# Attention and two expert layers on one core: last queries with the values moving, double transposes, and places that the plan keeps free

## The chip, the core and the metric

The kernel runs as one program on 1 core of a Trainium2 chip. Its engines are TensorE (PE, whose weight loads have a row of their own, PEld), VectorE (DVE), ScalarE (ACT), GpSimd (POOL) and SyncE (SP, which here only issues DMAs). The metric is the device time of one execution in microseconds; of several runs the median counts.

## What is computed

```python
def _attn_ref(q, k, v):            # q, k, v: [4, 8, 576, 64] float32
    q_rot, k_rot = (rotate(q), rotate(k))        # rotary embedding over the position
    scores = scale * np.matmul(q_rot, k_rot.transpose(0, 1, 3, 2))
    scores = scores - np.max(scores, axis=-1, keepdims=True)
    attn = np.exp(scores)
    attn = attn / (np.sum(attn, axis=-1, keepdims=True) + 1e-09)
    return np.matmul(attn, v)
def _moe_ref(x, w_in, w_out):      # 512 -> 2048 -> 512
    h = x @ w_in
    return (h * np.clip(h + 3.0, 0.0, 6.0) / 6.0) @ w_out
def _moe2_ref(x, w_in, w_out):
    h = x @ w_in
    return (h * (1.0 / (1.0 + np.exp(-1.702 * h)))) @ w_out
x = attn_out.transpose(0, 2, 1, 3).reshape(2304, 512)
return _moe2_ref(_moe_ref(x))
```

The weights come as float64. Nothing has to be written out between the three parts.

## The kernel before

**Precision.** Nearly every matrix product is made of numbers cut in two: a rounded high part (names ending in h) and the rest (names ending in l), and three matmuls (high by high, high by low, low by high) stand for one. A few products of attention take the full float32 matmul instead, which needs no low part: which ones is set by the numbers F00 to F21 of the table `C`, read by `full`.

**Attention.** The function `attention` goes over 16 pairs of heads (`pair`, 4 batches of 4 pairs). Of 576 queries 512 are four blocks of 128 for each head, and the last 64 of both heads share one block, whose rows 0 to 63 belong to one head and 64 to 127 to the other. For each block PE makes the scores (L554 for the four blocks, both heads at once, each on half of the array; L541 for the shared block), DVE takes the maximum (L527) and ACT the exponential (L529), which leaves the unnormed weights `P` (128 queries by 576 keys). To multiply by the values, PE transposes `P`, one key block after another (L609: 4 transposes of 128x128, one for each query block, into one of the 8 PSUM banks), ACT copies the high part out (L613), DVE the low part (L630), and PE multiplies (L636; L626 is the full float32 form; L621 the last, half-filled key block). The two halves of the product lie on partitions 0 to 63 and 64 to 127, and are added by `otmp` (ACT) and L643 (DVE) into `xf`.

**The shared last queries.** Their weights are transposed by L576 and L577 (into the banks `T8` and `E`), copied as `P8h` and `P8l` (L581 to L587), and multiplied in `pv8` (L596): the values are the weights of the array, 128 wide, and 64 columns of `P8h` or `P8l` move; 9 matmuls for each head, 18 in all. The halves are added by `otmp8` (ACT) and two L660 (DVE).

**The norm.** POOL spreads the reciprocal sums over 640 columns (`rx`: L400 twice, and L653 for the shared queries), PE transposes these in five pieces (L668 four, L669 one, into `E`), and DVE multiplies `xf` by them (L671, and L673 for the shared queries).

**First expert layer.** `moe1` works for each batch on 512 tokens (the last 64 queries of all batches are gathered in `xt` and run with batch 3 as a block of 256 columns, `xth` and `xtl`). Its 16 blocks of the hidden size go in 8 groups of two: L809 makes h, L814 (ACT) and L816 (DVE) the function, `gh` and `gl` (ACT, POOL) the two parts, L834 the second product, which L843 adds to `y`. The layer of batch b runs while attention of batch b+1 runs, and with batch 3 it runs alone. The first pass converts the weights from float64 (`weights`: SP loads `raw`, then ACT, POOL and DVE) and keeps them in DRAM (`w_hl`); later passes read them back by DMAs that POOL issues (L690).

**What sets the order.** All work is handed to a planner (`Plan`) as steps with an engine, an estimated time and a key. `Plan.run` plays the steps through by these estimates: whenever an engine is free, it takes the step with the lowest key whose inputs are done and whose places (buffers, PSUM banks) are free, and the order in which it took them becomes the order of the program. On the chip each engine then works through its own row strictly in that order and waits where an input is late. The numbers in `C` are keys, estimates and limits.

**The change of places.** After attention its pools (`apool`, `pp`) close, and two new pools take their memory: `y3pool` (yh, yl) and `tpool` (yback, xth, xtl, yt). Three 1 MB results of the first layer, kept in `y_dram`, come back as `yback` (L926), and are cut into `yh` and `yl` for the second layer. The steps of this part are handed over after the first `Plan.run`, and the planner does not know that their memory is attention's until then; the program's dependences still make them wait for it. The second layer (L1019, L1059, L1131) follows, alone on PE, to the end.

## Time and profile before

| | us |
|---|---|
| median of 3 runs | 1160.97 |
| lowest and highest | 1160.32, 1161.18 |
| the profiled execution | 1160.02 |
| its span, first to last instruction | 1158.2 |
| busy: PE, DVE, ACT, POOL | 1113.5, 729.5, 556.2, 650.5 |

The trace is of one profiled execution. The busy time of PE counts the modelled ends of pipelined matmuls, so a busy PE can still start its next matmul late; the distance from start to start of rows in a list in order of time is the surer price. Start times count from the start of the span. PEclk is the mean granted TensorE clock of a stretch, where 1.00 is 2.4 GHz.

### The profile page before, as it was taken

How to read it: one execution, taken by the hardware profiler on the slowest of the kernel's cores; microseconds unless marked ns; L12 is line 12 of the kernel's file. 1: busy time of each engine (PE TensorE's matmuls, PEld its weight loads, DVE VectorE, ACT ScalarE, POOL GpSimd, SP SyncE). 2: the span in 40 equal slices, each digit the busy share in tenths (PEclk: the TensorE clock that was granted, in tenths of full speed). 3: DMA queues.
4: the chain of work that ended last, by engine and by line, in shares of the span. 5: the costliest groups of instructions: out<-in, count | busy, mean ns of one | idle time of the engine just before them, and what ended most of it. 6: DMA issues, size and time to landing. Idle time of an engine off the chain costs nothing.

```text
span 1158.2 us, 17085 instructions
## 1 busy us (share of the span) xinstructions
PE 1113.5 (96%) x6408; PEld 918.1 (79%) x6408; DVE 729.5 (63%) x1131; ACT 556.2 (48%) x1106; POOL 650.5 (56%) x668
## 2 busy tenths in 40 slices
PE   5999999999999999999997999999999999999995
PEld 4667676776888888888886888888888888888884
DVE  5789777887756665566664343566556655565543
ACT  5787866566645554655544432253433334332330
POOL 5777777867753566353433444556745547464440
PEclk9999999999999999999998999999999999999998
DMA  3345565555543456443326543222012010110012
GB/s 90 90 133 169 178 192 188 190 187 184 177 132 103 129 149 182 126 142 109 109 74 218 191 138 109 74 65 81 19 55 61 31 55 19 56 55 25 30 74 91
DMA packets 58891, 129.73 MB, mean 112 GB/s; under 512 B 13752, under 2 KB 26808, under 8 KB 58040
## 3 DMA queue, kind: packets, MB, share of 16 engines
q1 hardware_dynamic: 44712, 78.13, 20.9%
q0 software_dynamic: 13824, 50.34, 14.6%
q8 instruction: 50, 0.82, 0.3%
q14 instruction: 33, 0.27, 0.1%
q10 hardware_dynamic: 272, 0.16, 0.0%
HBM read 103.97 MB, written 24.64 MB: 111 GB/s over the span
## 4 chain that ended last, share of the span: by engine, by line
PE 87%; DVE 5%; POOL 3%; ACT 2%; DMA 1%; issue 1%; SPq 0%; DVEq 0%; POOLq 0%
PE psum L834 17%; PE psum L1131 17%; PE psum L809 15%; PE psum L1019 11%; PE psum L1059 6%; PE psum L609 5%; PE psum L554 4%; PE psum L636 4%; PE psum L596 2%; PE psum L626 2%; DMA raw<-in_moe_w_in_dram 1%; PE psum L541 1%; POOL t L387 1%; DVE sc L527 1%; ACT P L529 1%
## 5 line engine op out<-in xcount | busy, mean ns | idle before, releaser
L387 POOL TENSOR_TENSOR gl<-t,gh 128x512 fp32r<-128x512 f32 (+1 forms) x144 | 183.1, 1275 | 146.3 <-ACT gh L397 126.3
L529 ACT ACTIVATE P<-psum,sc 128x576 f32<-128x576 f32 x144 | 105.4, 739 | 49.9 <-DVE sc L527 49.2
L527 DVE TENSOR_REDUCE sc<-psum 128x1 f32<-128x576 f32 x144 | 102.9, 751 | 30.0 <-PE psum L554 25.6
L1137 DVE TENSOR_TENSOR oacc<-oacc,psum 128x512 f32<-128x512 f32 x124 | 85.0, 685 | 49.0 <-PE psum L1131 47.5
L1131 PE MATMUL psum<-woh,gh 128*128 128x512 f32 x284 | 111.2, 391 | 0.0
L1131 PE MATMUL psum<-woh,gl 128*128 128x512 f32 x284 | 110.8, 390 | 0.0
L1131 PE MATMUL psum<-wol,gh 128*128 128x512 f32 x284 | 110.6, 390 | 0.0
L809 PE MATMUL psum<-xh,wih 128*128 128x512 f32 x256 | 107.1, 418 | 2.5 <-DVE t L816 2.5
L613 ACT ACTIVATE PTh<-psum 128x512 fp32r<-128x512 f32 (+2 forms) x160 | 88.0, 597 | 43.3 <-PE psum L609 42.6
L397 ACT ACTIVATE gh<-t 128x512 fp32r<-128x512 f32 (+1 forms) x136 | 82.2, 606 | 51.0 <-DVE t L1027 25.7
L834 PE MATMUL psum<-gh,woh 128*128 128x512 f32 x256 | 104.7, 409 | 0.2 <-DVE t L816 0.2
L843 DVE TENSOR_TENSOR y<-y,psum 128x512 f32<-128x512 f32 x112 | 76.4, 684 | 44.3 <-PE psum L834 43.6
L809 PE MATMUL psum<-xh,wil 128*128 128x512 f32 x256 | 101.7, 397 | 0.0
L809 PE MATMUL psum<-xl,wih 128*128 128x512 f32 x256 | 101.3, 396 | 0.0
L834 PE MATMUL psum<-gh,wol 128*128 128x512 f32 x256 | 100.4, 392 | 0.0
L834 PE MATMUL psum<-gl,woh 128*128 128x512 f32 x256 | 100.1, 391 | 0.0
L609 PE MATMUL psum<-ident,P 128*128 128x128 f32 (+1 forms) x640 | 87.6, 275 | 6.5 <-DVE PTl L630 3.0
L816 DVE SCALAR_TENSOR_TENSOR t<-t,psum 128x512 f32<-128x512 f32 (+1 forms) x80 | 49.7, 630 | 68.2 <-ACT t L814 67.9
L814 ACT ACTIVATE t<-psum,three 128x512 f32<-128x512 f32 (+1 forms) x80 | 50.5, 645 | 83.8 <-PE psum L809 66.4
L609 PEld LDWEIGHTS psum<-ident,P 128*128 128x128 f32 (+1 forms) x640 | 72.1, 135 | 23.4 <-DVE PTl L630 3.8
L630 DVE TENSOR_TENSOR PTl<-psum,PTh 128x512 fp32r<-128x512 f32 x100 | 67.0, 685 | 24.9 <-ACT PTh L613 24.4
L1027 DVE TENSOR_TENSOR t<-t,psum 128x512 f32<-128x512 f32 (+1 forms) x52 | 31.5, 605 | 78.6 <-ACT t L1025 76.0
(190 smaller groups left out, 3003.4 us busy)
## 6 DMA issues: line engine op xcount, KB each, us to landing
raw<-in_moe_w_in_dram SPq DMA_DIRECT2D x32, 512.0 KB, 3.9
raw<-in_moe_w_out_dram SPq DMA_DIRECT2D x32, 512.0 KB, 3.6
wih<-w_hl POOLq DMA_DIRECT2D x24, 512.0 KB, 4.4
wil<-w_hl POOLq DMA_DIRECT2D x24, 512.0 KB, 5.0
woh<-w_hl POOLq DMA_DIRECT2D x24, 512.0 KB, 4.3
wol<-w_hl POOLq DMA_DIRECT2D x24, 512.0 KB, 5.0
rawq<-in_q_dram SPq DMA_DIRECT2D x16, 256.0 KB, 3.1
rawk<-in_k_dram SPq DMA_DIRECT2D x16, 256.0 KB, 2.9
```

Source lines behind the costliest of these rows:

```text
L387: alts = [("Pool", ns or gps(n), lambda: nc.gpsimd.tensor_tensor(o(), i0(), i1(), op=op)), ("DVE", dve(n), lambda: nc.vector.tensor_tensor ...
L397: alts = {"ACT": ("ACT", act(n, psum), lambda: nc.scalar.activation(o(), i(), AF.Copy, scale=scale)), "DVE": ("DVE", dve(n, not psum), lam ...
L527: plan.op("DVE", dve(S), key + C["oM"], lambda: nc.vector.tensor_reduce(sc.t[:, i:i + 1], Sp.t[:, :, :HS], axis=AX.XY, op=ALU.max, negate= ...
L529: plan.op("ACT", act(S, True, True), key + C["oE"], lambda: nc.scalar.activation(halves(P[i].t), Sp.t[:, :, :HS], AF.Exp, bias=sc.t[:, i:i ...
L609: nc.tensor.transpose(T.t[:m, 0, c * 128:c * 128 + 128], P[hs + c].t[:, j * 128:j * 128 + m], ident)
L613: plan.op("ACT", act(512, True), key + C["oTh"], lambda T=T, hi=hi, m=m, fp=fp: nc.scalar.activation(hi.t.bitcast(F32) if fp else hi.t[:m] ...
L809: nc.tensor.matmul(hp.t[:, 0, :n], ww.t[:, cc, fs], xx.t[:, cc, :n], start=(cc == 0 and i == 0), stop=(cc == CC - 1 and i == 2))
L834: nc.tensor.matmul(yp.t[:, 0, :n], ww.t[:, a, cs], xx.t[:, a, :n], start=(i == 0), stop=(i == 3 * G - 1))
L843: plan.op("DVE", dve(n), ka + C["oY"], lambda yp=yp, y=y, c=c, n=n: nc.vector.tensor_tensor(y.t[:, c, :n], y.t[:, c, :n], yp.t[:, 0, :n], ...
L1019: nc.tensor.matmul(hp.t[:, 0, :n], ww.t[:, cc, fs], xx.t[:, cc, :n], start=(cc == 0 and i == 0), stop=(cc == CC - 1 and i == 2))
L1131: nc.tensor.matmul(op_.t[:, 0], xx.t[:, ts], ww.t[:, a, :], start=(i == 0), stop=(i == 3 * G - 1))
L1137: plan.op("DVE", dve(512), key, lambda op_=op_, tt=tt: nc.vector.tensor_tensor(oacc.t[:, tt], oacc.t[:, tt], op_.t[:, 0], op=ALU.add), r=[ ...
```

## The change

Six things change.

1. `tp`: key blocks 0 and 1, and 2 and 3, are transposed in one PE step of 8 transposes that takes two banks at once (`Ts`); block 4 keeps a step of 4.
2. `pv8`: the weights of the array are now `P8h` or `P8l` of a key block (128 queries, both heads), and the values move: 256 columns, 128 for each head, in two runs of the tile `vhl`. 9 matmuls replace 18. The result has the queries on partitions.
3. So the norm of the shared queries is a number for each partition: ACT multiplies one half out (`x8`, L664 of the new code), DVE multiplies the other and adds (L666), PE transposes the sum (L675), and two copies put it into `xf`. The steps `otmp8`, L660, L673, L669 and POOL's two small spreads for the shared queries go.
4. `Plan` notes until when steps hold a pool (`until`), and steps that write new tiles of `y3pool` and `tpool` may not be taken before attention's pools are free in the plan (`floors`).
5. The table `C` changes. For PE's work the counts of full float32 key blocks matter: batch 0 takes 3 and 2 (before 1 and 2) for its two heads, batch 1 takes 1 and 2 (before 2 and 2); in all 32 such matmuls instead of 28. `G0` lets the first weights load after the fifth score step instead of the ninth. The others move keys.
6. The estimates for the full float32 matmul (960 for 870) and of `pv8` change.

```diff
-     4.743, 'RQ': 15.555, 'RK': 13.622, 'TQ': 1.772, 'TK': -0.193, 'V': 0.921, 'PB': 11, 'RT': 1.0, 'oM':
+     'K0': 2.984, 'RQ': 23.454, 'RK': 23.04, 'TQ': 2.258, 'TK': 0.446, 'V': 1.653, 'PB': 11, 'RT': 1.0, 'oM':
...
-        o.t0 = max([d.end for d in deps if d.out], default=0.0)
+        o.t0 = max([d.end for d in deps if d.out] + [self.floors.get(b.pool, 0.0) for b in o.news], default=0.0)
...
+                    for b in o.bufs:
+                        self.until[b.pool] = max(self.until.get(b.pool, 0.0), o.end)
...
             def pv8():
-                for h in range(2):
-                    hs = slice(64 * h, 64 * h + 64)
-                    for j in range(5):
-                        lh = vhl.t[:, 5 * h + j].rearrange("p a d -> p (a d)")
-                        for i, x in enumerate((h8, l8) if j < 4 else (h8,)):
-                            nc.tensor.matmul(E.t[:, 0, 128 + 64 * h:192 + 64 * h], lh, x.t[:, j * 128:j * 128 + 128][:, hs],
-                                             start=(j == 0 and i == 0), stop=(j == 4))
+                for j in range(5):
+                    rh = vhl.t.rearrange("p (h j) a d -> p h j (a d)", h=2)[:, :, j]
+                    for i, x in enumerate((h8, l8) if j < 4 else (h8,)):
+                        nc.tensor.matmul(E.t[:, 0, 128:384].rearrange("p (h x) -> p h x", h=2), x.t[:, j * 128:j * 128 + 128], rh,
+                                         start=(j == 0 and i == 0), stop=(j == 4))
...
-                    T = Banks(plan, 1)
-
-                    def tp(T=T, j=j, m=m, hs=hs):
-                        for c in range(4):
-                            nc.tensor.transpose(T.t[:m, 0, c * 128:c * 128 + 128], P[hs + c].t[:, j * 128:j * 128 + m], ident)
-                    plan.op("PE", 4 * TR, key, tp, r=[P[hs + c] for c in range(4)], w=[T], mode=1)
+                    if j in (0, 2, 4):
+                        Ts = [Banks(plan, 1) for _ in range(2 if j < 4 else 1)]
+
+                        def tp(Ts=Ts, j=j, m=m, hs=hs):
+                            for i, T in enumerate(Ts):
+                                for c in range(4):
+                                    nc.tensor.transpose(T.t[:m, 0, c * 128:c * 128 + 128], P[hs + c].t[:, (j + i) * 128:(j + i) * 128 + m], ident)
+                        plan.op("PE", 4 * TR * len(Ts), key, tp, r=[P[hs + c] for c in range(4)], w=Ts, mode=1)
+                    T = Ts[j & 1]
...
-            plan.op("PE", 18 * 86, key, pv8, r=[vhl, h8, l8], w=[(E, 1)])
-            tmp8 = Buf(plan, pp, "otmp8", [64, 128], F32, 1)
...
+            plan.op("PE", 9 * 116, key, pv8, r=[vhl, h8, l8], w=[(E, 1)])
+            x8 = Buf(plan, pp, "x8", [128, 2, 2, D], F32, 1)
+
+            def o8(a):
+                return E.t[:, 0, 128:384].rearrange("p (h a d) -> p h a d", h=2, a=2)[:, :, a]
+            plan.op("ACT", act(128, True), key, lambda: nc.scalar.activation(
+                x8.t[:, 1], o8(1), AF.Copy, scale=sc.t[:, 26:27]), r=[(E, 1), (sc, "r")], w=[(x8, 1)])
+            plan.op("DVE", dve(128), key, lambda: nc.vector.scalar_tensor_tensor(
+                x8.t[:, 0], o8(0), sc.t[:, 26:27], x8.t[:, 1], op0=ALU.mult, op1=ALU.add), r=[(E, 1), (sc, "r"), (x8, 1)], w=[(x8, 0)])
...
-                nc.tensor.transpose(E.t[:, 0, 256:384], flat2(rxt(), 4), ident)
-            plan.op("PE", 5 * TR, key, tr, r=[rx], w=[R, (E, 2)], mode=1)
+            plan.op("PE", 4 * TR, key, tr, r=[rx], w=[R], mode=1)
+            plan.op("PE", TR, f(C["PV"] + C["P8"]) + 0.5, lambda: nc.tensor.transpose(
+                E.t[:, 0, 384:512], x8.t[:, 0].rearrange("p h d -> p (h d)"), ident), r=[(x8, 0)], w=[(E, 2)], mode=1)
...
+    over = max(plan.until.get(apool, 0.0), plan.until.get(pp, 0.0))
...
+        plan.floors = {y3pool: over, tpool: over}
```

How the rows of the engines move, at three places. First PE at the end of the last pair, where the shared queries are multiplied and the expert layer of batch 3 begins. Before:

```order
L621 MATMUL psum<-PTh,vhl 128x512
L668 MATMUL psum<-ident,t_6260 128x128 x4
L669 MATMUL psum<-ident,t_6260 128x128
L596 MATMUL psum<-P8h,vhl 128x64
L596 MATMUL psum<-P8l,vhl 128x64
```

After (line 598 is `pv8`, 675 the transpose of `x8`, 673 the four transposes of the norm, 817 the first matmul of the expert layer):

```order
L626 MATMUL psum<-PTh,vhl 128x512
L673 MATMUL psum<-ident,t_6089 128x128 x4
L598 MATMUL psum<-vhl,P8h 128x256
L598 MATMUL psum<-vhl,P8l 128x256
...
L675 MATMUL psum<-ident,x_6262 128x128
L817 MATMUL psum<-xh,wih 128x512
L817 MATMUL psum<-xl,wih 128x512
```

The 18 matmuls of 64 columns have become 9 of 256, the fifth transpose of the norm has gone, and the transpose of `x8` stands directly between `pv8` and the expert layer.

Second SP, the queue of loads where attention ends. Before:

```order
L907 DMA y_dram<-y 128x2048
L926 DMA yback<-y_dram 128x2048
L703 DMA raw<-in_moe_w_in_dram 128x2x512 x2
L711 DMA raw<-in_moe_w_out_dram 128x1024 x2
L926 DMA yback<-y_dram 128x2048 x2
```

After:

```order
L915 DMA y_dram<-y 128x2048
L711 DMA raw<-in_moe_w_in_dram 128x2x512 x2
L937 DMA yback<-y_dram 128x2048
L719 DMA raw<-in_moe_w_out_dram 128x1024 x2
L937 DMA yback<-y_dram 128x2048 x2
```

The first weights of the second layer (`raw`, in a pool that attention does not hold) now stand ahead of the first `yback`.

Third ACT at the same place (`xt` gathers the last queries, `xth` is its high part, `cvt` converts a weight, `t` is the function of the first expert layer). Before:

```order
L397 ACTIVATE xt<-xf 128x4x64
L397 ACTIVATE yh_6487<-yback 128x512
L397 ACTIVATE xth<-xt 128x1024
L397 ACTIVATE yh_6487<-yback 128x512
L714 ACTIVATE cvt<-raw 128x512
L814 ACTIVATE t<-psum,three 128x512 x2
```

After:

```order
L401 ACTIVATE xt<-xf 128x4x64
L722 ACTIVATE cvt<-raw 128x512
L401 ACTIVATE xth<-xt 128x1024
L722 ACTIVATE cvt<-raw 128x512
L822 ACTIVATE t<-psum,three 128x512 x2
L401 ACTIVATE yh_6344<-yback 128x512
L401 ACTIVATE gh<-t 128x512 x2
```

The step that needs `yback` has moved from ahead of `xth` to behind the two steps `t`.

## Rows read from the trace of the kernel before

**Rows 1.** Stretches: us; busy (instructions) of PE, PEld, DVE, ACT, POOL; clock, DMA share, GB/s.
```profile
20.00:100.00 80.00, 74.73 (x545) 55.27 (x546) 65.21 (x109) 66.59 (x149) 62.84 (x64) 1.00 0.35 106
300.00:600.00 300.00, 299.46 (x1797) 246.63 (x1796) 192.11 (x307) 161.19 (x330) 151.83 (x177) 1.00 0.43 126
600.00:640.00 40.00, 32.76 (x173) 27.77 (x171) 20.26 (x32) 18.28 (x33) 13.48 (x15) 0.87 0.60 208
640.00:750.00 110.00, 110.00 (x636) 97.12 (x635) 49.58 (x89) 35.45 (x70) 49.37 (x61) 1.00 0.41 126
```

**Rows 2.** PE in order of time: start, us, line, tile, shape, count. One pv8.
```profile
330.48 0.39 PE L809 MATMUL psum<-xh,wil 128*128 128x512 f32 x1
330.71 0.19 PE L596 MATMUL psum<-P8h,vhl 128*128 128x64 f32 x1
...
332.96 0.40 PE L809 MATMUL psum<-xl,wih 128*128 128x512 f32 x1
```

**Rows 3.** The chain that ended last: start, us, line, count. Matmuls of 256 columns.
```profile
802.19 4.97 PE psum L1059 x42
```

**Rows 4.** PE in order of time: steps of four and of eight transposes.
```profile
353.69 0.60 PE L609 MATMUL psum<-ident,P 128*128 128x128 f32 x4
...
354.36 0.39 PE L834 MATMUL psum<-gl,woh 128*128 128x512 f32 x1
...
355.51 1.03 PE L609 MATMUL psum<-ident,P 128*128 128x128 f32 x8
...
356.62 0.40 PE L834 MATMUL psum<-gl,woh 128*128 128x512 f32 x1
```

**Rows 5.** PE in order of time: two full float32 matmuls (four records) and the next.
```profile
178.78 1.93 PE L626 MATMUL psum<-PTh,rawv 128*64 128x512 f32 x4
180.65 0.50 PE L636 MATMUL psum<-PTh,vhl 128*128 128x512 f32 x1
```

**Rows 6.** Small steps (min/median/max ns), and two groups of the page (busy us, mean ns).
```profile
L583 ACT ACTIVATE P8h<-psum x16: 258/259/270, 42.6 to 608.0; 64x128 fp32r<-64x128 f32 x16
L587 DVE TENSOR_TENSOR P8h<-psum,P8h x16: 283/284/285, 42.9 to 608.3; 64x128 fp32r<-64x128 f32 x16
L529 ACT ACTIVATE P<-psum,sc 128x576 f32<-128x576 f32 x144 | 105.4, 739 | 49.9 <-DVE sc L527 49.2
L630 DVE TENSOR_TENSOR PTl<-psum,PTh 128x512 fp32r<-128x512 f32 x100 | 67.0, 685 | 24.9 <-ACT PTh L613 24.4
```

**Rows 7.** Where attention ends, in order of time: SP, ACT, PE [idle before <- releaser].
```profile
611.75 0.34 SPq L926 DMA_DIRECT2D yback<-y_dram  x1
...
616.80 0.63 ACT L397 ACTIVATE yh<-yback 128x512 fp32r<-128x512 f32 x1 [4.49 <-DMA yback<-y_dram]
...
618.43 0.39 PE L809 MATMUL psum<-xth,wih 128*128 128x256 f32 x1 [2.08 <-ACT xth L397]
620.86 0.58 PE L809 MATMUL psum<-xtl,wih 128*128 128x256 f32 x1 [2.04 <-POOL xtl L387]
...
631.17 0.50 PE L809 MATMUL psum<-xh,wih 128*128 128x512 f32 x1 [2.45 <-DVE t L816]
```

**Rows 8.** Busy time by stretch, as rows 1: three stretches with a lower clock.
```profile
616.00:632.00 16.00, 9.44 (x42) 7.91 (x41) 8.00 (x12) 8.49 (x15) 6.99 (x7) 0.79 0.66 214
632.00:636.00 4.00, 4.00 (x14) 3.25 (x13) 2.94 (x4) 1.05 (x2) 0.59 (x1) 0.57 1.05 371
187.00:192.00 5.00, 4.70 (x19) 3.48 (x21) 3.51 (x6) 3.34 (x7) 2.32 (x3) 0.67 1.02 346
```

**Rows 9.** PE's waits: line, waited for, us in total, times, longest.
```profile
PE psum L609 <- DVE PTl L630: 3.0, 3, 2.3
PE psum L596 <- DVE P8h L587: 0.7, 1, 0.7
```

**Rows 10.** A step of twenty transposes on PE, and the stretch around it.
```profile
47.81 2.42 PE L609 MATMUL psum<-ident,P 128*128 128x128 f32 x20
...
46.00:52.00 6.00, 5.90 (x52) 5.24 (x52) 5.06 (x12) 5.65 (x12) 4.96 (x5) 1.00 0.46 162
```

More of the change, by code (lines that the diff above doesn't have):

```diff
@@ L90, in __init__ @@
         self.psum = None
+        self.until = {}
+        self.floors = {}
     def op(self, eng, ns, key, fn, r=(), w=(), lat=None, alts=(), after=(), eager=False, kb=0, mode=0, port=()):
@@ L626, in pv @@
                             nc.tensor.matmul(O.t[0:64, 0], rv.t[:, h, j, :], hi.t.bitcast(F32), start=False, stop=False)
[L627 removed]
+                        pts.append((pv, 960, [rv, hi], 1))
                         continue
```

21 lines of the change are left out of this document (7 added, 14 removed), and 12 rows, old and new, of the table C.

## The prediction, made before the changed kernel was run

> **What bounds the kernel now.** I read the busy time by stretch first [rows 1]. From 300 to 600 us, where attention runs beside the first expert layer, PE is busy for 299.5 of 300 us and no other engine for more than 192; from 640 to 750 us PE is busy all the time. So in most of the span a microsecond of PE's own work is a microsecond of the result, and work of DVE, ACT or POOL costs nothing as long as it comes in time. Two places differ. In batch 0 (20 to 100 us) PE lacks 5.3 of 80 us, with ACT at 66.6 and DVE at 65.2. And from 600 to 640 us PE is busy for only 32.8 of 40 us, at a mean clock of 0.87: attention ends there, and the expert layer of batch 3 starts alone. In order of time this stretch shows the chain [rows 7]: SP issues the first `yback` at 611.75 (the place it needs is attention's until then), ACT stands before `yh` until its data lands at 616.80, `xth` stands behind `yh` in ACT's row, `xtl` behind `xth`, and PE waits 2.08, 2.04 and then 2.45 us (the last for a PSUM bank, since `t` came late on ACT as well). The clock falls too [rows 8].
>
> **The change part by part.** The sum is made against the profiled execution, 1160.0 us; the median is 0.95 us above it, which I add at the end.
>
> *pv8.* Before: from the start of the last matmul ahead of it at 330.48 to the second one behind it at 332.96 are 2.48 us; two plain steps of 0.23 (330.48 to 330.71) belong to the neighbours; 2.02 us are the price of 18 matmuls [rows 2]. After: 9 matmuls of 256 columns, each with its own weights. The nearest row is 42 such matmuls in 4.97 us, 0.118 each [rows 3], so 1.06 us. Saved per pair 0.96, in 16 pairs 15.3 us. What the trace does not show is a moving operand in two runs of 128 columns. Its cost lies between nothing and that of a matmul of 512 columns, 0.23 each or 2.07 for nine, which would save nothing. I take the lower end: the number of columns is that of the row, and PSUM is written in one run.
>
> *The norm of the shared queries.* One transpose goes, one comes: no change of PE's work. But the new transpose waits for ACT and DVE, and PE works strictly in order. The chain is one ACT step (0.26), one DVE step (0.28) and three handovers, which I estimate at 0.1 together: 0.65 us [rows 6]. In twelve of the 16 pairs the order has expert matmuls or a score step in between that cover it. In three pairs of batch 0 only five transposes stand there (five times 0.11, 0.55 us), and in two of them ACT has an exponential (0.74) ahead of its step; I charge 0.8 us for each, 2.4 in all (bounds 0.3 and 3). In the last pair nothing stands between: 0.65 us, with 96 matmuls of the expert layer queued behind it; it takes the place of the wait of `pv8` for `P8h`, 0.7 us [rows 9], since the order now puts two more value matmuls ahead of `pv8`. These two cancel. The POOL and DVE steps that go (POOL two, DVE three for one per pair) and the two copies that ACT gains are off the path, beside a busy PE; if that cover went, ACT's part would be two copies of about 0.26 each per pair, 8 us in all.
>
> *Double transposes.* A step of four from its start at 353.69 to the second matmul behind it at 354.36 takes 0.67 us, a step of eight from 355.51 to 356.62 takes 1.11 [rows 4]. The difference, 0.44, is four transposes of 0.11, and 0.67 less the matmul's 0.23 is again four of 0.11. So a step has no fixed price to speak of, and joining two saves PE nothing, though the planner charges 95 ns for each change between transposes and matmuls. I put 0. It costs something where PE must wait for two free banks; see the rivals.
>
> *Full float32.* Two such matmuls take from 178.78 to 180.65, 1.87 us, 0.94 each [rows 5]; the pair of high and low that each replaces takes 0.46. 32 instead of 28: 4 times 0.48, plus 1.9 us. DVE loses four low parts. All of batch 0's surplus (8) lies where PE lacked 5.3 us anyway and DVE was loaded, so a part may be hidden: bounds 0 and 3.8.
>
> *The end of attention.* Before it costs three waits of 2.08, 2.04 and 2.45, 6.6 us [rows 7], and work at the lower clock: in 632 to 636 us the mean clock is 0.57, so 43% of 4 us or 1.7 us are lost; in 616 to 632 us it is 0.79, and of the 3.4 us that this is worth about 2.3 fell on PE's work after 620.86 and the rest on its waits [rows 8]. Together 10.6 us. After: the loads of `raw` stand ahead of `yback` on SP and need no place of attention's, so `cvt`, which now stands before `xth` on ACT, has its data; it costs 0.6 us, not 4.5. `xth` is then done, by my estimate, about 2.6 us after the last transpose (two small copies, `xt`, `cvt`, `xth`), and PE wants it 5.5 us after (24 matmuls of 0.23). `xtl` stands on POOL behind one `xl` and four DMA issues as before, and ends some 6.1 us after: a wait of about 0.4. `yh` is now behind `t`, but `gh` is behind `yh`, so the second `t` (through `gl`) still hangs on `yback`: I work out that PE waits for a bank for 0.8 to 1.9 us where it waited 2.45. So 1.2 to 2.3 us are left, and up to 1.7 more if a wait of 1.9 us again lowers the clock. I take 8.0 saved, with bounds 6.6 and 9.4.
>
> *The new order.* Neither trace nor order tells what all other waits become. The ones of batch 0, and those of 2.29 us at 187 us with its lower clock after it (33% of 5 us, 1.7) [rows 8], [rows 9], can go or come anew. I put 0, with bounds of 5 either way.
>
> Sum: 1160.0 - 15.3 + 2.4 + 1.9 - 8.0 = 1141.0; with 0.95 for the median 1142.
>
> **A rule against the change.** A step of twenty transposes runs 2.42 us at a granted clock of 1.00, which is 2.4 GHz [rows 10]. The Trainium skill, in "TensorE: Matmul & The Clock Gate", Part 4 (PE-mode transpose), says that transposes do not count as activity of PE in the way matmuls do, and that the clock stays low in them. By that rule longer steps of transposes would pull the clock down, and this trace does not agree, at least not up to twenty in a row and beside matmuls.
>
> **The rivals.**
>
> 1. *The wait where attention ends stays.* Another late input takes `yback`'s place, for example the weights that POOL loads, or the four DMA issues ahead of `xtl`. For it: DMA is at its limit there (a share of 0.66 over 16 us, 1.05 after) [rows 8]. Against it: the order of SP and ACT shows the cause gone. It gives 1142 + 8 = 1150.
>
> 2. *The moving operand in two runs is slow*, and `pv8` saves nothing: 1142 + 15 = 1157, still faster. Against it: the columns per matmul are those of the row.
>
> 3. *More waits go than I count.* Batch 0 and the stretch to 200 us lose most of their idle time, since expert matmuls now start within the third pair: 1142 - 9 = 1133.
>
> 4. *Double steps starve PE of banks: slower than before.* Each of the 64 steps of eight (two in each of 32 heads) needs two of eight banks at once, and a bank comes free only when ACT and then DVE have read it. If each waits for one more low part on DVE (0.685) [rows 6], this is 64 times 0.685 or 44 us: 1142 + 44 = 1186. It decides from 19 / 64 = 0.30 us per step. Against it: before, PE waited 3.0 us for low parts in all, in three places [rows 9], and the order puts matmuls between most of the steps.
>
> 5. *The clock falls after each double step.* Before, a fall cost 1.7 us [rows 8]; 64 times 1.7 is 109 us: 1251. The twenty transposes at 1.00 [rows 10] speak against it. This is the result that the rule of the skill above would give.
>
> 6. *Nothing that counts*: the savings are eaten by new waits one by one, 1159 to 1163.
>
> **How the numbers follow.** Forecast (1137 to 1147) 0.60; rival 1 0.14; rival 2 0.05; rival 3 0.11; rival 4 0.05; rival 5 0.01; rival 6 0.04. The predicted time is 1142. The range leaves out rivals 2, 4, 5, 6 and the far edge of 3, and reaches from 1132 to 1151. A measurement of this kernel can tell about 0.2%, 2.3 us, from no change. Faster by more than that: forecast and rivals 1, 2 and 3, 0.90. Within: 0.04. Slower: rivals 4 and 5, 0.06.
>
> **What would show it.** In the changed profile nine matmuls of line 598 should take about 1.06 us; near 2.0 means rival 2. Around the first `xth` (near 600 us) PE should wait less than 2.5 us in all and the clock stay near 1.00; three waits of two microseconds mean rival 1. PE's waits for `PTl` and `PTh` at line 613 should stay under 6 us in all; 20 or more mean rival 4. The new transpose (line 675) should wait for DVE in few pairs, 3 us in all; if it waits in most, the cover that I read from the order isn't there. The busy time of PE should fall by about 13 us. The prediction is wrong above all if the planner's new order brings waits that neither the page nor the order can show.

## The result, and the profile after

The changed kernel takes **1146.8 us** (median of 4 runs, 1146.1 to 1147.7) against 1160.8 us of the kernel before, measured again beside it (median of 4 runs, 1160.3 to 1161.2): a ratio of 0.988, with an interval of 0.9863 to 0.9897. That is 14.0 us less. The forecast was 1142 us with a range of 1132 to 1151: the direction and the range hold, the point is 4.8 us too low. Every trace below is of one execution, and executions of one kernel differ by the granted clock (ten of the kernel `a_f0` below took from 1156.9 us at a mean clock of 0.992 to 1162.3 at 0.986), so the clock of a trace, and its price, belong to that execution.

Three rows by stretch of the changed kernel (columns as in [rows 1], the same stretches):

```profile
20.00:100.00 80.00, 70.60 (x467) 47.37 (x466) 61.07 (x92) 63.54 (x144) 60.84 (x55) 1.00 0.42 132
600.00:640.00 40.00, 38.30 (x216) 32.35 (x215) 20.89 (x33) 24.61 (x49) 18.10 (x21) 1.00 0.72 243
640.00:750.00 110.00, 109.74 (x631) 96.20 (x631) 56.93 (x102) 38.85 (x73) 46.82 (x53) 1.00 0.35 110
```

The reader sees two opposite moves. From 600 to 640 us PE is busy for 38.3 us where it was 32.8, and its clock is back from 0.87 to 1.00: that is the end of attention. From 20 to 100 us PE is busy for 70.6 us where it was 74.7, and no other engine is busier than before. Part of that is PE's own work, which has become less; but PE's waits from 25 to 150 us, by the list of waits, rise from 6.8 to 13.5 us: in batch 0 new waits have come.

Three marks on PE divide the span cleanly, and all later comparisons use them: the start of the first expert matmul behind attention (610.64 us before, 607.35 after), the start of the first second product behind it (638.42 and 625.69), and the end of PE's last matmul.

- Up to the first mark: 3.3 us gained.
- Between the first two: 27.8 us before, 18.3 after, 9.4 us gained.
- From there to PE's last matmul: 506.8 us before, 506.9 after. Nothing.

The span falls by the sum, 1158.2 to 1145.6. So three quarters of the gain come from the end of attention. The other place, where the forecast expected the larger part (15.3 less 2.4 and 1.9, 11 us), gave only 3.3.

**The end of attention.** SP, ACT and PE in order of time, to be held against [rows 7]:

```profile
597.52 1.42 SPq L711 DMA_DIRECT2D raw<-in_moe_w_in_dram  x2
607.66 0.34 SPq L937 DMA_DIRECT2D yback<-y_dram  x1
...
608.99 1.05 ACT L401 ACTIVATE xth<-xt 128x1024 fp32r<-128x1024 f32 x1
...
613.71 0.62 ACT L401 ACTIVATE yh<-yback 128x512 fp32r<-128x512 f32 x1
...
607.27 0.33 PE L675 MATMUL psum<-ident,x 128*128 128x128 f32 x1 [0.84 <-DVE x L666]
607.35 0.47 PE L817 MATMUL psum<-xh,wih 128*128 128x512 f32 x1
...
613.41 0.39 PE L817 MATMUL psum<-xtl,wih 128*128 128x256 f32 x1 [0.22 <-POOL xtl L391]
...
617.69 0.50 PE L817 MATMUL psum<-xh,wil 128*128 128x512 f32 x1 [0.48 <-DMA wil<-w_hl]
```

The loads of `raw` now stand ten microseconds ahead of `yback` on SP, `yh` stands behind `xth` on ACT and no longer waits, and PE's waits of 2.08, 2.04 and 2.45 us have become 0.22 and 0.48.

**The product for the last queries.** PE in order of time, the pair at 338 us, against [rows 2]:

```profile
338.22 0.28 PE L598 MATMUL psum<-vhl,P8h 128*128 128x256 f32 x1
...
339.18 0.28 PE L598 MATMUL psum<-vhl,P8h 128*128 128x256 f32 x1
339.30 0.39 PE L842 MATMUL psum<-gh,woh 128*128 128x512 f32 x1
339.53 0.40 PE L842 MATMUL psum<-gl,woh 128*128 128x512 f32 x1
```

Nine matmuls from 338.22 to 339.30: 1.08 us, and the next starts 0.23 us later. The 2.02 us of the 18 before hold one thing more. In the kernel before the 18 themselves take 1.92 us, from 330.71 to the start of the matmul behind them, and from that one to the next are 0.33 us where 0.23 is usual:

```profile
332.63 0.48 PE L809 MATMUL psum<-xh,wih 128*128 128x512 f32 x1
332.96 0.40 PE L809 MATMUL psum<-xl,wih 128*128 128x512 f32 x1
```

This tenth of a microsecond is part of the price of the 18, and a sum over their own line leaves it out.

**PE's waits**, five rows of the page of waits (line, waited for: us in total, times, longest):

```profile
PE psum L675 <- DVE x L666: 2.5, 3, 1.2
PE psum L613 <- ACT PTh L618: 2.5, 2, 2.3
PE psum L641 <- ACT PTh L618: 2.5, 2, 2.1
PE psum L498 <- ACT P L533: 2.4, 3, 1.8
...
PE psum L613 <- DVE PTl L635: 1.4, 2, 0.8
```

The first is the new transposition that waits for the scaled sum: 2.5 us in three places, 1.21 us at 98.30, 0.47 at 119.55 and 0.84 at 607.27 in the list in order of time. The others are waits for the softmax's output and for the transposed probabilities, which the new order has placed otherwise.

### The profile page after: what moved, and what is told of

Same layout as the page of the kernel before. It is cut to its first block, busy times and chain, and to the rows that moved or that the text cites. A ratio compares the mean times of both kernels' runs of the same rounds, so it can differ in the third digit from the quotient of the medians.

```text
span 1145.6 us, 16745 instructions
## 1 busy us (share of the span) xinstructions
PE 1099.8 (96%) x6264; PEld 900.8 (79%) x6264; DVE 715.1 (62%) x1096; ACT 571.9 (50%) x1157; POOL 625.4 (55%) x616
## 3 DMA queue, kind: packets, MB, share of 16 engines
q0 software_dynamic: 13824, 50.34, 14.6%
## 4 chain that ended last, share of the span: by engine, by line
PE 87%; DVE 4%; issue 2%; ACT 2%; POOL 2%; DMA 2%; SPq 0%; POOLq 0%; DVEq 0%; ACTq 0%
PE psum L1142 17%; PE psum L842 17%; PE psum L817 16%; PE psum L1030 11%; PE psum L1070 6%; PE psum L613 5%; PE psum L558 5%; PE psum L641 3%; PE psum L631 2%; PE psum L598 1%; PE psum L545 1%; DVE sc L531 1%; ACT P L533 1%; DMA wil<-w_hl 1%; PE psum L498 1%
## 5 line engine op out<-in xcount | busy, mean ns | idle before, releaser
L401 ACT ACTIVATE gh<-t 128x512 fp32r<-128x512 f32 (+1 forms) x144 | 86.6, 607 | 50.3 <-DVE t L1038 25.8
L391 POOL TENSOR_TENSOR wol<-cvt,woh 128x512 fp32r<-128x512 f32 x32 | 41.7, 1310 | 92.8 <-ACT woh L401 92.8
L613 PE MATMUL psum<-ident,P 128*128 128x128 f32 (+1 forms) x640 | 85.2, 276 | 6.1 <-ACT PTh L618 2.5
```

Of the source, the lines that this page charges most:

```text
L391: alts = [("Pool", ns or gps(n), lambda: nc.gpsimd.tensor_tensor(o(), i0(), i1(), op=op)), ("DVE", dve(n), lambda: nc.vector.tensor_tensor ...
L401: alts = {"ACT": ("ACT", act(n, psum), lambda: nc.scalar.activation(o(), i(), AF.Copy, scale=scale)), "DVE": ("DVE", dve(n, not psum), lam ...
L613: nc.tensor.transpose(T.t[:m, 0, c * 128:c * 128 + 128], P[hs + c].t[:, (j + i) * 128:(j + i) * 128 + m], ident)
```

## The experiments

For each kernel I read the same four numbers from its trace: the first mark, PE's waits up to it, the time that the lower clock took (one minus the granted clock times the length, summed over windows of 4 us from 24 to 604 us), and the distance between the two marks. "Work" is the first mark less waits less clock.

```
kernel       median   first mark   waits   clock   work    between the marks
before       1160.8     610.6       24.7     1.7    584.2   27.8
changed      1146.8     607.4       31.2     1.7    574.4   18.3
a_nofloor    1151.2     609.4       31.2     5.1    573.1   22.5
b_floor      1153.6     611.4       24.3     1.7    585.4   20.3
f_pv18       1161.4     621.2       31.1     1.7    588.4   18.3
a_single     1151.3     611.8       29.8     5.1    576.8   18.3
a_oldtable   1149.8     610.2       34.3     3.4    572.4   18.2
ao_single    1147.2     606.6       34.0     0.0    572.6   18.2
a_f0         1159.3     617.3       39.8     3.4    574.0   18.3
a_g0         1154.4     614.3       33.7     5.2    575.4   19.2
f_x8free     1160.6     623.2       38.5    12.0    572.7   18.3
f_x8id       1147.1     608.6       30.3     5.2    573.1   18.3
f_t1         1146.9     607.7       30.1     5.1    572.5   18.3
bf_pv8       1147.8     606.2       32.2     0.0    574.0   (other order)
```

The table is worth a look before the single runs. Work is 572 to 577 us in every kernel with nine matmuls, and 584 to 589 in every one with eighteen. What differs between kernels of equal work is waits and clock. On the chips on which these kernels ran, the kernel before took 1160.4 to 1161.4 us, so a microsecond between two medians is nothing. (Of the expectations, the last one names waits of 33.2 us for ao_single; these were counted to 2 us ahead of the mark.)

### The due time of attention's places: a_nofloor and b_floor

The edit takes the line away from the changed kernel, and puts it and what it needs alone into the kernel before.

```
a_nofloor (against the changed kernel)
-        plan.floors = {y3pool: over, tpool: over}
b_floor (against the kernel before)
+        self.until = {}
+        self.floors = {}
...
+        plan.floors = {y3pool: over, tpool: over}
```

> The changed kernel without the one line that gives the places of attention a due time (plan.floors), so the plan again believes that the back buffers and the expert activations have their room at once. Everything up to the end of attention is ordered as in the changed kernel or nearly so. Theory A (the end of attention was worth what the profiles say, 27.9 us from the first expert matmul behind attention to the first second product before, 18.3 us after): the waits of 2 to 2.5 us for the xl, xh and yh operands come back behind attention, the stretch is 26 to 28 us again, and the time is 8 to 10 us over the changed kernel, 1155 to 1157 us. Theory B (the new table alone put the order right, the due time does nothing): the order behind attention stays, and the time is 1146 to 1148 us.

Measured: 1151.2 us (ratio to before 0.991, 0.9894 to 0.9927), 4.4 us over the changed kernel. Between the marks stand 22.5 us against 18.3. SP and PE of this kernel, in order of time:

```profile
609.72 0.34 SPq L936 DMA_DIRECT2D yback<-y_dram  x1
610.12 0.94 SPq L711 DMA_DIRECT2D raw<-in_moe_w_in_dram  x2
...
616.37 0.38 PE L817 MATMUL psum<-xth,wih 128*128 128x256 f32 x1 [1.23 <-ACT xth L401]
618.86 0.38 PE L817 MATMUL psum<-xtl,wih 128*128 128x256 f32 x1 [2.11 <-POOL xtl L391]
```

`yback` is ahead of `raw` again, and two of the three old waits are back. Neither theory had the size: the due time is worth 4 us under the new table, not 8 to 10, and not nothing.

> The kernel before with only the due time for attention's places (plan.until, plan.floors) added; its table and everything else are its own, so the order up to the end of attention stays. Theory A (the prediction's step: 10.6 us lost at the end of attention, 1.2 to 2.3 left): the stretch from the first expert matmul behind attention to the first second product falls from 27.8 to 18 to 20 us, the time to 1151 to 1153 us. Theory B (as the changed kernel without its due time showed, with 22.5 us there against 18.3: the due time is worth 4 us and the rest came with the table): 1155 to 1158 us.

Measured: 1153.6 us (0.9935, 0.9918 to 0.9951), 7.8 us less than the 1161.4 us of the kernel before on the same chip. Between the marks 20.3 us against 27.8, up to the first mark nothing (611.4 against 610.6). So under before's own table the due time alone gives 7.5 us, nearer to theory A's mechanism; under the new table, whose order is better there anyway, 4. The 2 us that are still missing to 18.3 are not a wait. PE of this kernel, in order of time, and a stretch (columns as in [rows 1]):

```profile
609.29 0.30 PE L600 MATMUL psum<-P8h,vhl 128*128 128x64 f32 x1 [0.68 <-DVE P8h L591]
...
611.44 0.78 PE L813 MATMUL psum<-xh,wih 128*128 128x512 f32 x1
612.01 0.63 PE L813 MATMUL psum<-xl,wih 128*128 128x512 f32 x1
612.44 0.63 PE L813 MATMUL psum<-xh,wil 128*128 128x512 f32 x1
...
612.00:616.00 4.00, 4.00 (x14) 3.17 (x13) 3.56 (x7) 2.51 (x4) 4.00 (x6) 0.67 0.60 182
```

The matmuls from 612.01 on start 0.43 apart where 0.23 is usual, up to 614.6: PE runs at its lower level there, and the mean clock from 612 to 616 us is 0.67. That belongs to this execution and not to the due time: the kernel before has the same wait of 0.68 us ahead of the same 18 matmuls (at 608.61), and its matmuls behind them start 0.23 us apart.

### Eighteen matmuls again, nothing else: f_pv18

All engines keep the order of the changed kernel; only what PE issues in the place of the nine matmuls differs.

```
-                for j in range(5):
-                    rh = vhl.t.rearrange("p (h j) a d -> p h j (a d)", h=2)[:, :, j]
+                for h in range(2):
+                    for j in range(5):
+                        lh = vhl.t[:, 5 * h + j].rearrange("p a d -> p (a d)")
...
```

> The changed kernel with every engine's order of work kept as it is; only the instructions of the product for the last queries are those of before again: 18 matmuls a pair with the values as weights (here with 128 moving columns, so the values for the last queries are not the reference's) in place of nine with the values moving. Theory A (TensorE is the bound nearly everywhere, so the nine matmuls saved are saved in the time: 18.6 us of TensorE for them in the changed kernel, 31.4 before): 12 to 14 us over the changed kernel, 1158 to 1161 us. Theory B (much of the saving only turned into waits for the conversions of the first batch and for x8): 1151 to 1156 us, with 3 us or more less idle time on TensorE.

Measured: 1161.4 us (1.0002, 0.9992 to 1.0011), 14.6 us over the changed kernel, a little above theory A's range. Work rises from 574.4 to 588.4 us, waits stay (31.2 and 31.1). So in the changed kernel, with its order held, each of the nine saved matmuls is paid out in full; none of this saving turned into waits there.

### Another operand for the new transposition: f_x8free and f_x8id

```
f_x8free
-                E.t[:, 0, 384:512], x8.t[:, 0].rearrange("p h d -> p (h d)"), ident)
+                E.t[:, 0, 384:512], flat2(rxt(), 0), ident)
f_x8id
+                E.t[:, 0, 384:512], ident, ident)
```

> The changed kernel with every engine's order kept; the transposition that ends the last queries (the new one, of x8) reads the reciprocals, which are there long before, in place of x8, so it has no two operations of ScalarE and VectorE to wait for; the values for the last queries are not the reference's. Theory A (the new transposition's waits, 2.5 us by the page of waits, 6.8 us with the places where only the weight load shows it, lengthen the time): 1140 to 1144 us. Theory B (what waits there is late anyway, the next instruction would wait for the same engines): 1145 to 1148 us.

Measured: 1160.6 us (0.9997, 0.9985 to 1.0009), 13.8 us slower, which neither theory allowed. GpSimd's waits name the cause: the reciprocals that the transposition now reads lie in `t1`, the single buffer that the rope of the next pair needs, and they are held until the transposition has run (in one pair L673, which reads them last otherwise, starts at 100.49 and L675 at 104.62). From the groups of the two kernels, first the changed one:

```profile
L391 POOL TENSOR_TENSOR t<-rawq,tab 128x640 f32<-128x640 f32 x28 | 44.9, 1608 | 32.4 <-PE psum L673 24.5 <-DMA rawq<-in_q_dram 3.9 <-DVE P8h L591 3.4
```

then f_x8free:

```profile
L391 POOL TENSOR_TENSOR t<-rawq,tab 128x640 f32<-128x640 f32 x28 | 45.3, 1622 | 50.3 <-PE psum L675 39.5 <-PE psum L673 5.8 <-DMA rawq<-in_q_dram 4.0
```

In the profiled execution (1163.4 us, 2.9 over the median) the time went two ways. PE's waits rose by 7 us, and the lower clock took 12.0 us up to 604 us where it took 1.7. A stretch of f_x8free, columns as in [rows 1]:

```profile
132.00:136.00 4.00, 4.00 (x19) 3.49 (x19) 0.00 (x0) 0.00 (x0) 4.00 (x4) 0.50 0.22 65
```

PE is busy, all at the lower level (0.50 of 2.4 GHz), GpSimd is busy for 4 of 4 us, and DVE and ACT have nothing to do: which fits with the others standing behind GpSimd's rope.

> The same question as with the transposition that read the reciprocals, put without its flaw: the order of every engine is kept, and the last queries' transposition reads the identity, which is a constant and holds no buffer (the values for the last queries are not the reference's). In that earlier kernel GpSimd's rope of the next pair waited 39.5 us for this transposition, since the reciprocals lie in the buffer t1 that the rope needs next. Theory A (the loss of 14 us there came from holding t1 longer; the wait for x8 itself has a price): 1141 to 1145 us. Theory B (it came from t1, and the x8 wait costs nothing): 1145 to 1148 us. Theory C (t1 had no part; a transposition that comes early does harm by itself): 1158 to 1162 us.

Measured: 1147.1 us (0.988, 0.9859 to 0.9901), as the changed kernel. Theory C falls: f_x8free differs from this kernel by the operand of one transposition alone, so the 13.8 us there came from holding t1. Between A and B the run does not decide, although its time is in B's range, for it does not take the wait away. The transposition in f_x8id, in two places:

```profile
117.77 0.33 PE L675 MATMUL psum<-ident 128*128 128x128 f32 x1 [0.46 <-DVE x L666]
608.47 0.33 PE L675 MATMUL psum<-ident 128*128 128x128 f32 x1 [0.85 <-DVE x L666]
```

It waits for the sum `x8` (L666) as before, 0.46 and 0.85 us where the changed kernel has 0.47 and 0.84, though it no longer reads it; the list of waits of f_x8free has the same 1.3 us. The likely reason is the PSUM bank `E`: the transposition writes into it, L664 and L666 read from it, and the edit leaves that. Only the longest of the three waits, 1.21 us, is gone, and not by the operand. In the changed kernel it stands behind a weight conversion of 1.81 us that DVE runs ahead of L666:

```profile
96.18 1.81 DVE L731 SCALAR_TENSOR_TENSOR cvt<-raw,cvt 128x512 int32<-128x512 int32 x1
...
98.30 0.33 PE L675 MATMUL psum<-ident,x 128*128 128x128 f32 x1 [1.21 <-DVE x L666]
```

In f_x8id the same conversion took 0.69 us, and L666 was done in time. So what this wait costs in the result no run here shows.

### The buffer t1: f_t1

The reciprocals of the first two batches are put into a part of `xt` that is idle there; every engine's order stays.

```
+            if b < 2:
+                def own():
+                    if xt.t is None:
+                        xt.alloc()
+                rx.alloc = own
...
```

> The changed kernel with every engine's order kept, except that in the first two batches the reciprocals that the transposition at L673 reads lie in a part of xt that is idle there, and no longer in t1, so the rope of the next pair need not wait for that transposition (GpSimd waits 24.5 us for it in the changed kernel, 10.5 us of it in one place at 117 us). Theory A (this single buffer ties the pairs of the first batch together, and is where the change's gain in the first batch went): TensorE's idle time from 25 to 150 us falls from 13.5 to 5 to 9 us, the time to 1137 to 1142 us. Theory B (GpSimd has slack there, and the pairs are tied by something else): 1145 to 1148 us.

Measured: 1146.9 us (0.9881, 0.9863 to 0.9898): theory B, although GpSimd's wait for this transposition is gone, as its group shows:

```profile
L391 POOL TENSOR_TENSOR t<-rawq,tab 128x640 f32<-128x640 f32 x28 | 45.2, 1617 | 9.7 <-DMA rawq<-in_q_dram 4.0 <-DVE P8h L591 3.4 <-PE psum L682 1.4
```

PE's waits fall by 1.1 us. (The lower clock takes 3.4 us more in the profiled execution; the last section shows why that is no price of the edit.) So the buffer has slack in the changed order. Holding it longer costs 14 us, giving it back early brings nothing.

### Steps of four transposes, and the old table: a_single, a_oldtable, ao_single

```
a_single
-                    if j in (0, 2, 4):
-                        Ts = [Banks(plan, 1) for _ in range(2 if j < 4 else 1)]
+                    T = Banks(plan, 1)
a_oldtable
-C = {'T0': 45.984, 'D1': 15.009, ...
+C = {'T0': 9.62, 'D1': 13.312, ...
ao_single: both of these
```

> The changed kernel with one step of four transposes for each key block, in one PSUM bank, as before the change; all else of the change stays. Theory A (a step of eight saves nothing: eight transposes take the time of twice four, and it holds two banks at once): 1144 to 1148 us, the waits for PTh and PTl at the value products no longer than in the changed kernel. Theory B (two blocks in one step save the entry into the transposes' form, some 0.2 us for each of the 64 steps that go away): 1152 to 1160 us. Theory C (the steps that ask for two banks starve the others): 1138 to 1143 us, with 3 us or more less waiting for PTh.

Measured: 1151.3 us (0.9919, 0.9904 to 0.9933), 4.5 us slower than the changed kernel; theory A fails by 3 us, theory B's lower edge is missed by 1.

> The changed kernel with the table of numbers of before: all of the change but its table. Theory A (the code's edits carry the gain, the table's part is small: nine matmuls -12.8 us, the end of attention -4 to -9): 1143 to 1150 us. Theory B (any order that was not sought for this very code pays in waits of the first batch, as three kernels with one number or one step changed did, by 4 to 10 us up to the end of attention): 1150 to 1158 us, with 4 us or more over the changed kernel before the first expert matmul behind attention. Theory C (the old table fits the old code so closely that nothing is left): 1159 us or more.

Measured: 1149.8 us (0.9906, 0.9891 to 0.992), 3.0 us over the changed kernel: at the upper edge of theory A. All that the change does but its table gives 11 of the 14 us.

> The changed kernel with the table of before and with transposes in steps of four, one bank each: beside the kernel before with only the due time it has the product and the end of the last queries as changed, beside the changed kernel with the old table it lacks only the steps of eight. Both of these have first expert matmuls behind attention at 611.4 and 610.2 us. Theory A (the nine matmuls give 14 us, and the steps of eight, which take two banks and a step of 0.9 us at once, give them back in the first batch): 1140 to 1145 us, TensorE's idle time from 25 to 150 us 6 to 9 us. Theory B (the steps of eight are worth nothing either way, the loss comes with the pairs' chain as the last queries now close it): 1148 to 1153 us, idle time 13 us or more.

Measured: 1147.2 us (0.9885, 0.9865 to 0.9906), between the two theories, and with 20 us of waits between 25 and 300 us (11.7 and 8.5) no case for A's reason. Under the old table the steps of eight cost 2.6 us by the medians (the intervals of the two ratios touch, and the traces differ by the clock, 3.4 against 0.0 us, with equal work and waits), under the new one they save 4.5. A price of the steps themselves would have one sign. What differs besides is the order that the planner makes around them.

### One or two numbers of the table: a_f0 and a_g0

```
a_f0:  'F00': 3 -> 1, 'F10': 1 -> 2
a_g0:  'G0': 5 -> 9
```

> The changed kernel with the table's numbers of blocks in full fp32 in the first batch as before (F00 from 3 to 1, F10 from 1 to 2; 28 full fp32 matmuls in place of 32). Theory A (the four more fp32 matmuls cost TensorE 4 x 0.48 us, and the first batch is bound by its chain of softmax and conversions, so that this work fell into waits or lengthened it alike): 1144 to 1148 us, TensorE busy 1.5 to 2 us less. Theory B (the first batch waits more in the changed kernel because the fp32 blocks changed its order): 1139 to 1143 us, and the idle time of TensorE from 25 to 150 us goes from 13.4 back towards 6.2 us.

Measured: 1159.3 us (0.9987, 0.9972 to 1.0001). Work stays at 574 us, but waits rise by 8.6 us and the first mark by 10: less full float32 work, and almost all of the gain of the change gone. Neither theory. (The profiled execution took 1157.1 us, 2.2 under the median, so the trace shows some 10 of the 12.5 us.)

> The changed kernel with the table's lead of the expert groups (G0) at 9 as before in place of 5, so the first expert group and its weight conversions start later in attention. Theory A (in the changed kernel the early weight conversions on VectorE, of 1.06 and 1.81 us, stand ahead of the short operations that attention's chain waits for, and the first batch so lost some 7 us more to waits): the idle time of TensorE from 25 to 150 us falls from 13.4 to 6 to 9 us, the time to 1139 to 1143 us. Theory B (the waits there come from the chain of the first batch itself, whatever the lead): idle time and time stay, 1145 to 1149 us. Theory C (the expert work is filler that covers the waits; with it later there is less to fill): slower, 1150 to 1156 us.

Measured: 1154.4 us (0.9938, 0.9923 to 0.9953). First mark 6.9 us later, waits and clock 2.5 and 3.5 us more. Theory A fails outright; C has the size, though not its reason, since the waits from 25 to 150 us are 12.9 us against 13.5.

One number of the table costs 7.6 us (a_g0), two cost 12.5 (a_f0), most of it in waits and clock. It does not follow that every plan from a point that was not sought pays: the whole old table costs 3.0 us (a_oldtable), and with steps of four 0.4 (ao_single).

### Before's own order with nine matmuls: bf_pv8

If the planner's order is what makes waits, the order of before, with the new product put into it by hand, should keep its few.

```
             def pv8():   (as in the changed kernel, in before's place)
...
+            def last8():
+                nc.tensor.transpose(E.t[:, 0, 384:512], x8.t[:, 0].rearrange("p h d -> p (h d)"), ident)
+                for h in range(2):
+                    hs = slice(64 * h, 64 * h + 64)
+                    nc.vector.tensor_copy(xf.t[hs, hp, 512:], E.t[hs, 0, 384:512][:, hs])
```

> The kernel before with the due time for attention's places, in the order of every engine that this kernel has (so before's own order up to the end of attention), into which the changed product for the last queries is put: nine matmuls with the values moving in the place of the 18, the scaled sum on ScalarE and VectorE in the place of the old copy and additions, its transposition and copies in the place of the last product with the reciprocals. Steps of four transposes, before's table. The kernel with the same work but planned anew from the same table took 1147.2 us, with its first expert matmul behind attention at 606.6 us and 33.2 us of idle TensorE up to there; the one with only the due time 1153.6 us, 611.4 and 24.3 us. Theory A (the order of before was sought with its own code and waits little; any plan made anew pays 5 to 14 us in waits up to the end of attention, and that is where the gain of the nine matmuls went): idle stays at 23 to 27 us, the first expert matmul comes at 597 to 600 us, the time is 1139 to 1143 us, below both kernels. Theory B (the waits come from the new end of the last queries or from the first batch's own chain, whatever the order): idle rises to 30 us or more, the time is 1145 to 1149 us.

Measured: 1147.8 us (0.9881, 0.9865 to 0.9898), waits 32.2 us against 24.3 in b_floor: theory B, and A falls. PE's waits in the kernel with only the due time (b_floor), whose order this is:

```profile
PE psum L613 <- DVE PTl L634: 3.1, 3, 2.3
PE psum L613 <- ACT P L533: 1.5, 2, 1.2
PE psum L613 <- ACT PTh L617: 1.4, 2, 0.7
```

and in bf_pv8:

```profile
PE psum L611 <- DVE PTl L632: 2.5, 3, 1.8
PE psum L847 <- DVE y L856: 2.4, 4, 0.9
...
PE psum L683 <- DVE x L670: 1.7, 1, 1.7
PE psum L611 <- DVE xf L686: 1.7, 3, 0.6
PE psum L611 <- ACT P L533: 1.5, 2, 1.2
PE psum L611 <- ACT PTh L615: 1.4, 2, 0.7
```

The old waits stand nearly as they stood. Beside them are new ones for `x` and `xf`, the end of the last queries as it is now, and for `y`, which DVE delivers late. So a part of the new waits comes with the edit even in before's order: with PE's work 11.4 us shorter, the first mark moved by 5.3 only. How much of them, `y`'s lateness above all, comes from the way I put the copies behind the transposition on DVE, I can't tell apart.

No version beats the changed kernel by more than a run's spread; ao_single, f_t1, f_x8id and bf_pv8 equal it.

## Why the prediction was right, and where it was off

**The end of attention** (forecast 8.0, bounds 6.6 to 9.4): 9.4 us, at the upper bound. The mechanism is shown twice, by b_floor (7.5 us with the due time alone) and a_nofloor (two of the waits and the old order on SP return). The waits left were put at 1.2 to 2.3 us; the trace shows 0.22 and 0.48, and the clock stayed at 1.00. Not all of it is the due time: under the new table taking it away costs 4.1 us between the marks (22.5 against 18.3), so part of the 9.4 comes with that table's order. Rival 1 is refuted.

**pv8** (forecast 15.3): the row of the pair at 338 us fits the estimate, 1.08 us where 1.06 was expected, and rival 2 is refuted: a moving operand in two runs costs nothing. But over all 16 pairs the saving is smaller. Summed from start to start, with the waits that the trace shows taken out, the product's own lines take 31.4 us before and 18.6 after. To this comes what the operation behind starts late: before, some 0.09 us in twelve pairs and 0.06 in four, after, 0.06 in two. Together 14.0 us are saved, not 15.3, and f_pv18 gives the same in the changed order: 14.0 us of PE's work, 14.6 in the time. The term was mis-sized because a pair without any disturbance was taken for all: the mean after is 1.17 us a pair, not 1.06, where the mean before is near the 2.02 of [rows 2].

**The new transposition's wait** (forecast 2.4 us in three pairs): 2.5 us in three places. That the sum is met is luck, since the places are others. In the three pairs of batch 0 where only five transposes stand in between, 0.8 us each was charged; these wait 0.13, 0.13 and 0.47 us. The third pair of the batch, which has expert and score matmuls in between and was put at nothing, waits 1.21, for DVE stood in a weight conversion of 1.81 us, which the forecast left out. In the last pair 0.84 us stand where 0.65 was expected; the steps on ACT and DVE take 0.37 and 0.35 us, not the 0.26 and 0.28 of [rows 6]. The wait for `P8h` there is gone, as foreseen. What these waits cost in the time is not shown (f_x8id).

**Double transposes** (forecast 0): the lines of the transposes take 68.8 us before and 69.6 after, start to start. No saving on PE, as worked out from [rows 4]. Rival 4 is refuted: waits for `PTh` and `PTl` at line 613 are 3.9 us, under the 6 that I set. Rival 5 as well: up to 604 us the lower clock takes 1.7 us in both kernels. Rivals 3 and 6 fall too: waits rose instead of going, and 14 us are left. The Trainium skill, in "TensorE: Matmul & The Clock Gate", Part 4 (PE-mode transpose), which says that transposes don't count as activity in the way matmuls do, is not borne out as a price of longer steps here. One stretch of the changed kernel is less clear, and is shown in the last section.

**Full float32** (forecast plus 1.9): the fp32 line rises by 3.1 us, the pairs that it replaces fall by 1.4. Plus 1.7, near the forecast.

**The new order** (forecast 0, bounds of 5 either way): this is the second step that was off. PE's waits up to the first mark rise by 6.5 us, from 24.7 to 31.2, of which 2.5 are the new transposition and 4.0 others. It lies within the bounds, but not at 0. The step that failed is that a plan made anew was priced at no waits on balance. Two sources are seen: a plan can lose much by one or two numbers of the table (a_g0, a_f0: 7.6 and 12.5 us in the time), and the edit, as it was placed by hand, brings waits even into the order of before (bf_pv8, 24.3 to 32.2 us). Which of them made the 6.5 us of the changed kernel stays open. That the single buffer `t1` is where they come from is refuted (f_t1).

So, between the profiled executions (1141.0 forecast, 1147.7 measured), 6.7 us are to be explained: pv8 1.3, the order 4.0, the transposes 0.7, the matmuls of the scores 1.8 (80.8 us before, 82.6 after, which the forecast left out), less 1.4 at the end of attention, 6.4 in all. The rest is small and lies in other lines, with both signs. The range held because its bounds for the new order were wide enough for the larger part of this; 1146.8 us is at the upper edge of the forecast's own 1137 to 1147. That the profiled execution of the changed kernel lay above its median, and not below as that of before, makes the point look better by 1.8 than the sum was.

## What to carry to other kernels

Divide the span at marks that both kernels have, and write the stretch ahead of a mark as work, waits and clock: here work kept to two narrow bands, some 5 us wide, in fourteen kernels, and most surprises were in the other two. An edit to a kernel whose order was sought should be priced with some microseconds of new waits, not with zero plus or minus, for the order was sought with the old work in it; that PE's work had been the cover of somebody's delay is my reading and not shown. And a run that is meant to take a wait away must be looked at twice: for whether the wait is gone (in f_x8id it was not), and for what else the edit holds (in f_x8free a transposition that read another tile cost 14 us through one buffer that lived 3 to 5 us longer in the pairs of the first batch).

## What the runs showed of the hardware that I had not expected

**A wait can cost more than itself, by some 1.7 us, and the same wait does so in one execution and not in another.** The lower clock took 0, 1.7, 3.4 or 5.1 us up to 604 us in the traces of thirteen of the fourteen kernels, and 12.0 in that of f_x8free. One such step in the changed kernel, by stretch (columns as in [rows 1]):

```profile
192.00:196.00 4.00, 2.02 (x13) 1.75 (x13) 3.97 (x7) 4.00 (x10) 1.52 (x2) 0.86 0.71 200
196.00:200.00 4.00, 4.00 (x15) 3.21 (x14) 3.22 (x5) 1.30 (x3) 1.70 (x2) 0.71 0.78 289
```

and PE in order of time there:

```profile
190.54 1.09 PE L613 MATMUL psum<-ident,P 128*128 128x128 f32 x8
193.89 2.45 PE L613 MATMUL psum<-ident,P 128*64 128x128 f32 x12 [2.25 <-ACT PTh L618]
...
196.56 0.63 PE L842 MATMUL psum<-gl,woh 128*128 128x512 f32 x1
196.99 0.63 PE L842 MATMUL psum<-gh,wol 128*128 128x512 f32 x1
```

Eight transposes, a wait of 2.25 us, twelve transposes, and then matmuls 0.43 us apart until 198.3: a wait of 2.25 us that cost 4. The same place in f_x8id, whose PE row is the same there:

```profile
194.00 1.82 PE L613 MATMUL psum<-ident,P 128*64 128x128 f32 x12 [2.25 <-ACT PTh L618]
...
192.00:196.00 4.00, 1.90 (x14) 1.60 (x15) 4.00 (x6) 4.00 (x10) 1.41 (x2) 1.00 0.67 204
196.00:200.00 4.00, 4.00 (x21) 3.06 (x21) 3.92 (x7) 1.31 (x3) 1.81 (x2) 1.00 0.94 312
```

The same wait, the same matmuls around it, and the clock stays at 1.00. Two other waits of the changed kernel, 1.78 us at 131.47 and 2.09 at 240.56, have the full clock behind them there; in the traces of f_x8id and f_t1 the same waits (1.78 us each, 2.06 and 2.08) are followed by the lower level. So the length of a wait does not decide it. The 3.4 us more of lower clock in the traces of f_x8id and f_t1 are no price of their edits, and differences of 2 to 5 us between the traces of two kernels of equal work should not be read as more; what sets the level off stays open.

**From 64 to 256 columns the number of matmuls counts, hardly their width.** In f_pv18 a matmul of 128 columns takes 0.11 us from start to start, as one of 64 columns did before (18 in 2.02 us); one of 256 columns takes 0.12 (338.22 to 339.30, nine). At 512 columns it is 0.23. PE of f_pv18 in order of time:

```profile
346.52 0.28 PE L599 MATMUL psum<-P8h,vhl 128*128 128x128 f32 x1
346.63 0.45 PE L843 MATMUL psum<-gh,woh 128*128 128x512 f32 x1
```

This is why exchanging the operands nearly halves the product's time: half as many matmuls, each four times as wide, at nearly the same price. The narrow ones also delay what comes behind: the first matmul of 512 columns takes 0.31 to 0.32 us to the next behind 18 of 64 columns, 0.28 to 0.29 behind 18 of 128 (f_pv18), and 0.23 behind nine of 256.
